# A stabilised linear-attention kernel with a gated feed-forward part: its instruction list ordered anew, with new engines for some 270 steps and new PSUM banks

## The chip, the cores and the metric

One core of a Trainium2 chip runs the whole program. It has a matrix engine (PE, with PEld for its weight loads), a vector engine (DVE), a scalar engine (ACT), a general engine (POOL), and a queue engine (SP) that here only issues transfers. All transfers run on the core's 16 DMA engines. Every engine takes its own instructions strictly in the order in which they are written, and semaphores hold an instruction until what it needs is there. The metric is the time of one execution on the device in microseconds (us); a lower time is better.

## The reference

For 4 batches of 8 heads, 768 time steps and a head size of 40 the first part is a recurrence with exponential gates. The second takes the result as rows of 320 numbers, and computes a gate by a causal convolution of 5 taps, a product with a weight matrix, and a product with a second one.

```python
for t in range(S):
    m_new = np.maximum(f_gate[:, :, t] + m, i_gate[:, :, t])
    f_stab = np.exp(f_gate[:, :, t] + m - m_new)
    i_stab = np.exp(i_gate[:, :, t] - m_new)
    m = m_new
    C = f_stab[:, :, None, None] * C + i_stab[:, :, None, None] * np.einsum('bhd,bhe->bhde', vt, kt)
    n = f_stab[:, :, None] * n + i_stab[:, :, None] * kt
    h_tilde = np.einsum('bhde,bhe->bhd', C, qt)
    denom = np.maximum(np.abs(np.einsum('bhd,bhd->bh', n, qt)[:, :, None]), 1.0)
    o = 1.0 / (1.0 + np.exp(-o_gate[:, :, t]))
    y[:, :, t] = o * h_tilde / denom
# x: y as [batch, time, 320]; xp: x with 4 rows of zeros ahead
gate_pre = sum(conv_w[k] * xp[:, k:k + S, :] for k in range(5))
out = (1 / (1 + np.exp(-gate_pre)) * (x @ w_val)) @ w_out
```

## The kernel before

The 768 steps are cut into 6 tiles (j) of 128 rows, each tile into 4 batches (b). A unit u = 4j + b covers one batch of a tile, with its 8 heads side by side, and has two halves of 64 steps, g = 2u and 2u + 1. Inside a half the recurrence is written as matrix products; between halves a state of 40 x 41 numbers per head is carried on.

The program is one long list, `PLAN`, of 1447 steps. A step such as `probs.18=V` names a function, its numbers and its engine (V for DVE, A for ACT, P for POOL, S for SP), and `scores.18#5` names a matrix step and the PSUM bank (0 to 7) that it writes. The functions are called in the order of the list, and each engine gets its instructions in that order. The list alone decides the order of work, which of several engines does a copy or an elementwise step, and which of the eight banks a matrix step fills. No planner runs when the kernel is built.

The steps that the change and the later sections touch, with the lines of the profile:

- Loads on SP: `ldq` (L390) and `ldk` (L394) bring q and k of a tile into `nat`, `ldv` (L403) brings v into `vc` (`ldv.j.0` for the first half, `ldv.j.1` for the second), `ldo` (L406) the output gate, `wld` (L775) the weights. `sog`, `soa`, `sig_` and `sia` (L443 to L460) carry the cumulated gates through DRAM into `ra` and `la`.
- Splitting q and k: `mx` (L469, ACT) takes the largest value, `scs` (L480 to L485, DVE) makes a scale, `hi` (L497, L499, L501) and `lo` (L506, always DVE) write a high and a low half-precision part into one of three `stk` buffers.
- Turning them: for tiles 0 and 1 PE transposes (`trp`, L523) and `trc` (L527) copies out of PSUM. For tiles 2 to 5 it is `trd` (L518), a transposing transfer on SP, 32 in all: one for q into `tq` and one for k into `tk` for every unit.
- A half g: `args` (L543, PE), `expo` (L547, ACT), `scores` (L555, PE, reads `tk` and `tq`), `probs` (L560, DVE), `keyw` (L568, DVE or POOL), `heads` (L595, PE, reads `vc`), `state` (L578, PE), `stout` (L587, copies the state into `vc`).
- A unit: `norm` (L610 to L615), `rsm` (L619), `gate` (L622, DVE), which ends the attention of a unit; `xeh`, `xel` (L633, L637) split a piece of it, `xtr` (L644, L646, PE) turns it, and `xhc`, `xcc`, `x3c`, `xlo` (L659 to L671) copy and split it.
- The second part, by tile: `cva`, `cvp` (L694, L700) and `cv3` (L708, L710) for the convolution, `sigm` (L721) for the gate, `val` (L731, PE), `zmul` (L736), `zhi` and `zlo` (L740, L745), `outp` (L753, PE), `obc` (L757) into one of two `ob` buffers, and `od` (L760), which stores it. For the last tile, steps from `cva` to `zlo` run in two parts of two batches.
- Weights: `wcv` (L789 to L803), `whi` and `wlo` (L816 to L834) turn the loaded 64-bit weights into two parts; `cpk` (L399) copies k into `kp`.

The choice of engine and bank lies in the loop that ends the function:

```python
for step in PLAN.split():
    step, _, b_ = step.partition("#")
    step, _, e = step.partition("=")
    name, *num = step.split(".")
    steps[name](int(b_) if b_ else e, *(int(n) if n.isdigit() else n for n in num))
```

Of the kernel before, what the change touches and what calls it, by code (L numbers as in the profile page):

```python
# [34 lines left out]
ldv.0.0=S mx.1.0.1=A ldq.2.1=S wcv.0.5=A ldo.0=S trp.0.1.1#5 trp.0.1.0#6 trp.0.2.1#7 ldk.2.0.2=S trc.0.1.0=V args.1#0
trc.0.1.1=V args.0#2 args.2#3 scs.0.0.2.2.3.3=V scs.0.0.2.1.2.3=V scs.0.0.2.3.4.3=V trp.0.2.0#1 zcmp.1.0=V
scs.1.0.2.0.4.0=V scs.0.0.2.1.2.2=V scs.0.0.2.3.4.2=V scs.0.0.2.2.3.2=V scs.1.0.2.0.4.1=V expo.1=A wcv.0.3=V
hi.1.1.1=P trp.0.3.0#4 expo.2=A hi.1.0.1=A args.3#6 keyw.2=P scores.2#5 trc.0.3.0=V scores.1#0 expo.0=A zcd.1=P
args.5#3 wld.1.1=S probs.2=V trc.0.2.1=A wcv.0.4=P scores.0#4 wcv.5.6=V heads.2#2 keyw.0=P lo.1.0.1=V chh=A expo.5=A
# [867 lines left out]
```

## Time and profile before

| | |
|---|---|
| three runs | 241.88, 243.8, 245.06 us; median 243.8 us |
| the profiled execution | 244.12 us, of which the span of its instructions is 242.3 us |
| busy share of the span | DVE 88%, PE 84%, ACT 71%, POOL 53% |
| DMA engines, busy share from 50 to 178 us | 1.18 |

The busy share of an engine is the time with an instruction in it, over the span. A DMA share over 1 means that packets of more than 16 transfers overlap. The chain of waits follows the work that ended last back to the start, and gives at each step what released it. `SPq` in a row is the time that the queue engine spent on issuing a transfer.

### The profile page before, as it was taken

The page shows a single profiled execution, that of the slowest core. Times are in us where ns is not written, and L with a number is a line of the kernel's source. Part 1 is how long each engine was busy: PE and PEld are TensorE (multiplying, and loading weights), DVE is VectorE, ACT ScalarE, POOL GpSimd, SP SyncE. Part 2 cuts the span into 40 slices and gives each one's busy share as a digit, 9 for nine tenths or more (in the row PEclk, how much of TensorE's full clock was granted, in tenths as well). Part 3 has the DMA queues.
Part 4 walks back from the last instruction along what each step waited for, and adds up shares of the span by engine and source line. Part 5 has one row for each costly group of instructions (what it writes and reads, how often), then busy time and mean ns, then how long its engine had stood idle before and what let it go on. Part 6 is the DMA issues. An engine that isn't in the chain of part 4 may idle for free.

```text
span 242.3 us, 6769 instructions
## 1 busy us (share of the span) xinstructions
PE 202.8 (84%) x2544; PEld 171.6 (71%) x2544; DVE 212.7 (88%) x459; ACT 171.9 (71%) x407; POOL 128.4 (53%) x209
## 2 busy tenths in 40 slices
PE   0079469987887699889997985999989989999994
PEld 0045368976776687667965974986879768898994
DVE  7999839999999669996999998897899989998982
ACT  7987928968988569894888965965958268536331
POOL 8942717658968873876766634123518112615330
PEclk9999979999999679995999999999999999999999
DMA  7998897699899999999899999999940330010223
GB/s 122 156 190 122 125 157 146 122 155 146 136 183 148 159 173 172 154 153 167 152 167 164 131 224 167 168 168 221 130 101 4 88 86 27 0 43 14 81 84 108
DMA packets 143832, 31.58 MB, mean 130 GB/s; under 512 B 139576, under 2 KB 142840, under 8 KB 143800
## 3 DMA queue, kind: packets, MB, share of 16 engines
q1 hardware_dynamic: 143696, 31.05, 84.4%
q8 instruction: 20, 0.33, 0.6%
q14 instruction: 12, 0.10, 0.1%
q10 hardware_dynamic: 104, 0.10, 0.1%
HBM read 17.87 MB, written 4.23 MB: 91 GB/s over the span
## 4 chain that ended last, share of the span: by engine, by line
PE 39%; DVE 32%; DMA 9%; ACT 6%; issue 6%; SPq 5%; POOL 1%; DVEq 0%; ACTq 0%; POOLq 0%
PE bank L595 9%; PE bank L753 9%; PE bank L731 6%; DVE stk L506 5%; PE bank L578 5%; DVE pk L560 4%; PE bank L710 3%; DVE sg L736 3%; SPq L394 2%; DMA la<-gda 2%; PE bank L555 2%; DMA vc<-in_v_dram 2%; PE bank L543 2%; DMA tk<-stk 2%; DMA raw<-in_moe_w_val_dram 2%
## 5 line engine op out<-in xcount | busy, mean ns | idle before, releaser
L595 PE MATMUL bank<-vc,pk 128*64 128x41 f32 (+1 forms) x768 | 57.0, 238 | 8.5 <-DMA vc<-in_v_dram 3.6
L595 PEld LDWEIGHTS bank<-vc,pk 128*64 128x64 f32 (+1 forms) x768 | 51.5, 145 | 13.0 <-ACT dm L547 4.0
L578 PE MATMUL bank<-vc,pk 128*40 128x41 f32 (+1 forms) x704 | 38.1, 212 | 1.3 <-DVE xc L663 0.7
L568 POOL TENSOR_TENSOR pk<-kp,dm 128x320 f32<-128x320 f32 (+1 forms) x32 | 25.8, 807 | 22.8 <-ACT dm L547 13.8
L560 DVE SCALAR_TENSOR_TENSOR pk<-bank,cmp,dm 128x512 f32<-128x512 f32 x48 | 34.7, 739 | 3.3 <-PE bank L555 2.2
L578 PEld LDWEIGHTS bank<-vc,pk 128*40 128x40 f32 (+1 forms) x704 | 33.1, 126 | 4.6 <-POOL cdt L863 1.8
L547 ACT ACTIVATE dm<-bank 128x512 f32<-128x512 f32 x48 | 28.0, 597 | 11.1 <-PE bank L543 8.6
L506 DVE SCALAR_TENSOR_TENSOR stk<-nat,scl,stk 128x320 f16<-128x320 f32 x48 | 33.7, 708 | 0.1
L700 DVE SCALAR_TENSOR_TENSOR bank<-xc,cwt,bank 128x512 f32<-128x512 f32 (+1 forms) x42 | 27.8, 671 | 0.6 <-ACT bank L694 0.3
L501 POOL TENSOR_SCALAR stk<-nat,scl 128x640 f16<-128x640 f32 x22 | 18.6, 848 | 14.7 <-issue 6.1
L469 ACT ACTIVATE junk<-nat 128x320 bf16<-128x320 f32 x48 | 22.5, 468 | 2.0 <-DMA nat<-in_k_dram 1.5
L619 POOL TENSOR_TENSOR rs<-sg,den 128x320 f32<-128x320 f32 x17 | 12.4, 735 | 20.8 <-DVE den L615 14.4
L543 PE MATMUL bank<-ra,la 120*128 120x512 bf16 x48 | 18.5, 404 | 5.5 <-DMA la<-gda 2.5
L753 PE MATMUL bank<-woh,zh 128*128 128x320 f32 x72 | 19.3, 324 | 3.7 <-ACT ob L757 2.8
L523 PE MATMUL bank<-idh,stk 128*120 128x128 f16 x128 | 9.8, 232 | 14.2 <-DVE stk L506 13.8
L555 PEld LDWEIGHTS <-tk 120*128 120x128 f16 x384 | 15.6, 102 | 7.1 <-issue 3.6
L555 PE MATMUL bank<-tq,tk 120*128 120x64 f16 x384 | 18.4, 199 | 2.2 <-DMA tk<-stk 0.9
L523 PEld LDWEIGHTS <-stk 128*120 128x120 f16 x128 | 9.1, 144 | 15.1 <-DVE stk L506 14.2
L753 PE MATMUL bank<-wol,zh 128*128 128x320 f32 x72 | 18.4, 309 | 0.0
L587 ACT COPY vc<-bank 40x328 f32<-40x328 f32 x31 | 13.1, 425 | 7.3 <-PE bank L578 6.8
L721 ACT ACTIVATE sg<-sg 128x2816 f32<-128x2816 f32 (+2 forms) x7 | 12.4, 1764 | 7.1 <-DVE sg L700 7.1
L497 ACT ACTIVATE stk<-nat,scl 128x640 f16<-128x640 f32 x20 | 16.2, 825 | 1.1 <-DVE scl L482 0.4
(169 smaller groups left out, 507.1 us busy)
## 6 DMA issues: line engine op xcount, KB each, us to landing
nat<-in_q_dram SPq DMA_DIRECT2D x24, 160.0 KB
vc<-in_v_dram SPq DMA_DIRECT2D x12, 320.0 KB
sg<-in_o_gate_dram SPq DMA_DIRECT2D x6, 640.0 KB
out_dram<-ob SPq DMA_DIRECT2D x24, 160.0 KB
nat<-in_k_dram SPq DMA_DIRECT2D x10, 320.0 KB
raw<-in_moe_w_val_dram SPq DMA_DIRECT2D x5, 160.0 KB
raw<-in_moe_w_out_dram SPq DMA_DIRECT2D x5, 160.0 KB
nat<-in_k_dram SPq DMA_DIRECT2D x4, 160.0 KB
```

What stands on the lines that cost most here:

```text
L469: A.activation(junk, part(j, x, i), AF.Abs, accum_out=amx[j % 2][:, x, i : i + 1])
L506: V.scalar_tensor_tensor(t[:, :, c : c + D], part(j, x, i), scl[j % 2][:, x, i : i + 1], t[:, :, 0:D], op0=ALU.mult, op1=ALU.subtract,)
L523: nc.tensor.transpose(t[0:K3, h], stk[(j * B + i) % NSTK][:, x, h, 0:K3], id16)
L543: nc.tensor.matmul(psd, la[:, p, j % SL, b], ra[:, :, j % SL], start=True, stop=True)
L547: A.activation(dms[g % NDM], late["psd", g], AF.Exp)
L555: nc.tensor.matmul(pss[:, h], tk[h], tq[:, h], start=True, stop=True)
L560: V.scalar_tensor_tensor(pks[g % NPK][:, :, 0:L], late["pss", g], cmp_[j % 2][:, p, b : b + 1], dms[g % NDM], op0=ALU.mult, op1=ALU.mult,)
L568: eng[e].tensor_mul(pks[g % NPK][0:n, :, L:], kp[0:n, p, b * H : (b + 1) * H], dms[g % NDM][0:n, :, L - 1 : L].to_broadcast([n, H, D]),)
L578: nc.tensor.matmul(pc[n0 : n0 + D, h], pks[g % NPK][0:n, h, L:], vc[j % 2][0:n, p, b * H + h], start=True, stop=True)
L595: nc.tensor.matmul(ph[p * L : (p + 1) * L, h], pks[g % NPK][0:n, h, 0:L], vc[j % 2][0:n, p, b * H + h], start=True, stop=True,)
L700: V.scalar_tensor_tensor(o, xc[j % 2][:, c, b0:b1, t : t + P], cwt[:, c, t : t + 1], pv, op0=ALU.mult, op1=ALU.add)
L753: nc.tensor.matmul(po, z, w, start=(i == 0), stop=(i == len(mm) - 1))
```

## The change

`PLAN` alone is replaced: the same 1447 steps in a new order, with the engine of 272 steps and the bank of 268 matrix steps changed. No function, buffer or shape changes. Of the engines' steps 108 leave DVE (54 to POOL, 54 to ACT) and 94 come to it (47 from POOL, 47 from ACT), while 30 pass from POOL to ACT and 30 from ACT to POOL; ten more pass between SP and ACT or POOL, all of them transfers or copies of `kp`.

```diff
 PLAN = """
-zvc.1=P ldf=A ldi=S zkp=V ldq.0.0=S zero.sel=P fsel.0=P ldk.0.0.1=S zero.id=V fsel.1=P zero.tl=V fid=P ldk.0.1.2=S
...
+zrst.1=P ldi=A ldf=S zstk.0=V zkp=V zvc.1=P ldq.0.0=S ldk.0.0.1=S zero.io=P zcmp.0.1=P ldq.0.1=S zero.oh=P
...
```

Three places show what moves.

**The first values of v, on SP.** `L403` loads v of tile 0; the first of the two rows before is `ldv.0.1`, the second `ldv.0.0`. Before:

```order
L449 DMA gda0_141<-gsp0_137 48x1x64
L403 DMA vc0_82<-in_v_dram 64x32x40
L456 DMA ra_86<-gdg0_139 24x8x64
L460 DMA la_85<-gda0_141 24x4x64 x2
L399 DMA kp_81<-nat0_79 64x640
L403 DMA vc0_82<-in_v_dram 64x32x40
L390 DMA nat0_79<-in_q_dram 128x8x40
```

In the change:

```order
L775 DMA raw0_148<-in_moe_w_val_dram 64x640
L456 DMA ra_86<-gdg0_139 24x8x64
L460 DMA la_85<-gda0_141 24x4x64 x2
L403 DMA vc0_82<-in_v_dram 64x32x40 x2
L775 DMA raw1_149<-in_moe_w_val_dram 64x640
```

The two halves now stand together behind the gates, the first half ahead, and the copy of `kp` between them has gone to ACT.

**The transposing transfers of tile 2, on SP.** `stk` holds the split rows, `tq` and `tk` the turned ones that `scores` reads; `nat` is the input of a later tile. Before:

```order
L518 DMA_TRANSPOSE tq0_100<-stk1_109 128x8x128
L518 DMA_TRANSPOSE tq0_100<-stk2_110 128x8x128
L518 DMA_TRANSPOSE tq0_100<-stk0_108 128x8x128
L394 DMA nat1_80<-in_k_dram 128x16x40
L460 DMA la_85<-gda1_142 24x4x64
L394 DMA nat1_80<-in_k_dram 128x16x40
L518 DMA_TRANSPOSE tk0_97<-stk0_108 128x8x128
L518 DMA_TRANSPOSE tk2_99<-stk2_110 128x8x128
L518 DMA_TRANSPOSE tq0_100<-stk2_110 128x8x128
L403 DMA vc0_82<-in_v_dram 64x32x40 x2
```

In the change:

```order
L390 DMA nat1_80<-in_q_dram 128x8x40
L394 DMA nat1_80<-in_k_dram 128x16x40 x2
L390 DMA nat1_80<-in_q_dram 128x8x40
L460 DMA la_85<-gda1_142 24x4x64
L403 DMA vc0_82<-in_v_dram 64x32x40
L518 DMA_TRANSPOSE tk2_99<-stk2_110 128x8x128
L518 DMA_TRANSPOSE tq0_100<-stk2_110 128x8x128
L403 DMA vc0_82<-in_v_dram 64x32x40
L518 DMA_TRANSPOSE tq0_100<-stk0_108 128x8x128
L518 DMA_TRANSPOSE tk0_97<-stk0_108 128x8x128
L460 DMA la_85<-gda1_142 24x4x64
```

The inputs of tile 3 now stand ahead of the first transposing transfer of tile 2, and the transfers for q and k of one unit stand side by side, nearer to the `scores` that read them.

**The last two units, on DVE.** `L622` is `gate`, the end of a unit's attention; behind its last row the engine has only the second part of the layer. Before:

```order
L619 TENSOR_TENSOR rs2_123<-sg_84,den2_120 128x320
L622 TENSOR_TENSOR x2_126<-bank5_73,rs2_123 128x320
L671 TENSOR_TENSOR xl0_596<-xc0_87,xh0_594 128x2x128
L619 TENSOR_TENSOR rs1_122<-sg_84,den2_120 128x320
L757 COPY ob1_131<-bank4_72 128x320
L633 CAST xe2_129<-x2_126 128x64
L700 SCALAR_TENSOR_TENSOR bank7_75<-xc1_88,cwt_96,bank7_75 128x256
L622 TENSOR_TENSOR x1_125<-bank6_74,rs1_122 128x320
L633 CAST xe1_128<-x1_125 128x64
```

In the change:

```order
L619 TENSOR_TENSOR rs1_122<-sg_84,den2_120 128x320
L740 CAST zh_615<-sg_84 128x512
L622 TENSOR_TENSOR x1_125<-bank1_69,rs1_122 128x320
L757 COPY ob0_130<-bank5_73 128x320
L619 TENSOR_TENSOR rs2_123<-sg_84,den2_120 128x320
L622 TENSOR_TENSOR x2_126<-bank2_70,rs2_123 128x320
L700 SCALAR_TENSOR_TENSOR bank7_75<-xc0_87,cwt_96,bank7_75 128x512
```

The two units end closer together, the splitting casts behind them (`L633`) have left DVE, and 50 rows of DVE follow the last `gate` where 45 followed it before.

## Rows read from the trace of the kernel before

**Rows 1.** The page's busy time of each engine with its share of the span, and from its table of 40 equal slices the busy tenths of PE and DVE, of the DMA engines, and the bytes that these moved.

```profile
PE 202.8 (84%) x2544; PEld 171.6 (71%) x2544; DVE 212.7 (88%) x459; ACT 171.9 (71%) x407; POOL 128.4 (53%) x209
...
PE   0079469987887699889997985999989989999994
...
DVE  7999839999999669996999998897899989998982
...
DMA  7998897699899999999899999999940330010223
GB/s 122 156 190 122 125 157 146 122 155 146 136 183 148 159 173 172 154 153 167 152 167 164 131 224 167 168 168 221 130 101 4 88 86 27 0 43 14 81 84 108
```

**Rows 2.** Busy time of each engine in stretches: bounds and length in us, then busy us with the number of instructions for PE, PEld, DVE, ACT and POOL, the granted PE clock, the DMA share, GB/s.

```profile
20.00:40.00 20.00, 15.00 (x212) 12.08 (x211) 14.92 (x36) 13.65 (x27) 9.83 (x14) 0.91 0.97 143
...
50.00:178.00 128.00, 112.57 (x1565) 94.62 (x1563) 114.43 (x242) 100.14 (x242) 77.53 (x117) 0.95 1.18 164
140.00:160.00 20.00, 16.16 (x293) 14.64 (x292) 17.77 (x43) 14.76 (x44) 6.40 (x10) 1.00 1.15 179
...
178.00:242.30 64.30, 59.45 (x562) 52.43 (x559) 55.08 (x118) 31.57 (x74) 20.95 (x30) 0.99 0.18 55
220.00:242.30 22.30, 19.11 (x136) 18.28 (x135) 15.98 (x36) 7.41 (x15) 6.91 (x8) 0.98 0.21 74
```

**Rows 3.** The chain of waits: its shares by engine, and its two longest pieces behind the first tiles that are transfers (start us, us, what).

```profile
PE 39%; DVE 32%; DMA 9%; ACT 6%; issue 6%; SPq 5%; POOL 1%; DVEq 0%; ACTq 0%; POOLq 0%
...
145.85 3.83 DMA out_dram<-ob
...
169.69 4.35 DMA tk<-stk
```

**Rows 4.** The first `heads`: issues on SP and the copy on DVE from the timeline (start us, us, engine, line, what; in brackets the engine's idle time just before and what ended it), then a row of the table of waits (us in total, times, longest).

```profile
20.19 0.67 SPq L403 DMA_DIRECT2D vc<-in_v_dram  x1
...
25.37 0.67 SPq L403 DMA_DIRECT2D vc<-in_v_dram  x1
...
28.55 5.48 SPq L394 DMA_DIRECT2D nat<-in_k_dram  x1
...
36.34 0.92 DVE L587 COPY vc<-bank 40x328 f32<-40x328 f32 x2 [3.94 <-PE bank L578]
...
PE bank L595 <- DMA vc<-in_v_dram: 3.6, 1, 3.6
```

**Rows 5.** Groups by line and shape (line, engine, operation, tiles, shapes, count | busy us, mean ns of one | idle us before and its releasers).

```profile
L506 DVE SCALAR_TENSOR_TENSOR stk<-nat,scl,stk 128x320 f16<-128x320 f32 x48 | 33.7, 708 | 0.1
...
L497 ACT ACTIVATE stk<-nat,scl 128x640 f16<-128x640 f32 x20 | 16.2, 825 | 1.1 <-DVE scl L482 0.4 <-DMA tk<-stk 0.4 <-DMA tq<-stk 0.3
...
L637 POOL TENSOR_TENSOR xe<-x,xe 128x64 fp32r<-128x64 f32 x9 | 4.3, 477 | 8.4 <-DVE xe L633 5.1 <-PE bank L731 3.1
L527 DVE COPY tq<-bank 120x1024 f16<-120x1024 f16 x6 | 4.1, 683 | 0.9 <-PE bank L523 0.8
...
L671 DVE TENSOR_TENSOR xl<-xc,xh 128x256 fp32r<-128x256 f32 x8 | 3.4, 424 | 0.0
...
L637 DVE TENSOR_TENSOR xe<-x,xe 128x64 fp32r<-128x64 f32 x15 | 3.1, 215 | 0.4 <-ACT xe L633 0.3
L499 DVE TENSOR_SCALAR stk<-nat,scl 128x640 f16<-128x640 f32 x6 | 3.1, 545 | 1.0 <-DMA tk<-stk 1.0
...
L399 DVE COPY kp<-nat 64x640 f32<-64x640 f32 x2 | 1.4, 692 | 0.1
...
L799 DVE TENSOR_TENSOR wf<-we,wa 128x320 f32<-128x320 f32 x1 | 0.7, 687 | 0.0
```

**Rows 6.** The low part `lo` on DVE beside POOL, from the timeline (columns as in rows 4).

```profile
29.07 1.08 DVE L506 SCALAR_TENSOR_TENSOR stk<-nat,scl,stk 128x320 f16<-128x320 f32 x1
...
29.08 0.73 POOL L568 TENSOR_TENSOR pk<-kp,dm 128x320 f32<-128x320 f32 x1
...
31.40 0.53 DVE L506 SCALAR_TENSOR_TENSOR stk<-nat,scl,stk 128x320 f16<-128x320 f32 x1
```

**Rows 7.** The transposing transfers: two of tile 2 issued one behind the other and the `scores` that wait for them, from the timeline; then how long one takes SP to issue (min/median/max ns, first and last start us).

```profile
69.62 4.79 SPq L518 DMA_TRANSPOSE tk<-stk  x2
...
77.80 0.41 PE L555 MATMUL bank<-tq,tk 120*128 120x64 f16 x8 [0.88 <-DMA tk<-stk]
...
L518 SPq DMA_TRANSPOSE tq<-stk x16: 1232/1282/4537, 61.6 to 175.2; - x16
L518 SPq DMA_TRANSPOSE tk<-stk x16: 1232/1342/5760, 69.6 to 192.2; - x16
```

**Rows 8.** Sizes of the transfers from the page's list of issues (engine, count, KB each), and the longest wait of ACT and DVE for a store to end (table of waits).

```profile
nat<-in_q_dram SPq DMA_DIRECT2D x24, 160.0 KB
vc<-in_v_dram SPq DMA_DIRECT2D x12, 320.0 KB
sg<-in_o_gate_dram SPq DMA_DIRECT2D x6, 640.0 KB
...
ACT ob L757 <- DMA out_dram<-ob: 3.3, 2, 2.7
...
DVE ob L757 <- DMA out_dram<-ob: 1.4, 1, 1.4
```

More of the change, by code (lines that the diff above doesn't have):

```diff
@@ L35 @@
[L35 to L39, printed above, removed]
@@ L65 @@
-keyw.15=P gate.4=V xtr.2#3 expo.16=A args.18#5 probs.14=V rsm.5=P wcv.2.5=A ldv.2.0=S expo.18=A wcv.2.2=V heads.14#4
-wlo.1.0=P stout.11=V ldv.2.1=S mx.3.3.1=A gate.5=V state.15#7 mx.3.1.1=A xel.3=V lo.2.2.1=V ldk.4.0.2=S heads.15#4
-xhc.2=A wcv.2.3=V keyw.18=P norm.6.0=A xcc.2=V state.13#0 wcv.2.4=V norm.7.0=A xcb.6=A mx.3.0.1=A cpk.2.0.1=P
-scores.18#5 stout.13=V scores.16#6 x3c.2=A xtr.3#2 wcv.2.6=V stout.15=A wld.3.1=S keyw.16=P args.17#0 hi.2.3.1=A
-norm.6.1=V args.19#3 scores.17#7 xeh.4=A xlo.1=P scs.3.0.2.0.4.0=V expo.17=A norm.6.2=V probs.16=V rsm.7=P wld.3.0=S
@@ new lines @@
+ldv.2.0=S xtr.1#2 stout.12=A wcv.2.2=V args.15#3 norm.4.2=V lo.2.0.1=V hi.2.1.0=A scores.13#7 rsm.5=P trd.2.0.1=S
+probs.13=V mx.3.0.1=A rsm.4=P gate.5=V wcv.2.5=A state.14#7 whi.1.0=V expo.15=A cdd.1.0=P heads.13#0 lo.2.1.1=V
+zcd.0=P xcc.0=A gate.4=V mx.3.2.1=A trd.2.0.0=S cdd.1.2=P scores.14#6 keyw.15=P stout.14=A xtr.3#3 probs.14=V
+scores.15#1 xhc.3=A cpk.2.0.0=P args.16#5 xeh.4=A args.17#7 probs.15=V mx.3.1.0=A ldv.2.1=S heads.14#6 xel.4=P xcc.3=A
+keyw.13=V cpk.2.1.0=P expo.17=A lo.2.1.0=V heads.15#6 x3c.1=A xcc.1=A x3c.3=A mx.3.3.1=A stout.11=V trd.2.1.0=S
@@ new lines @@
+wcv.3.5=A ldq.4.1=S sigm.0.0.4=A xel.7=P rsm.8=V wlo.2.2=P ldk.4.0.2=S probs.20=V ldq.4.0=S gate.9=V args.23#6
+gate.8=V heads.20#2 lo.3.1.0=V xeh.8=P lo.3.2.0=V xlo.5=P ldv.3.1=S scores.22#1 zmul.0.1.0.4=V heads.21#2
+zmul.0.0.0.4=V x3b.7=P trd.3.1.0=S keyw.21=P expo.23=A state.22#4 probs.22=V mx.4.1.0=A xlo.4=P scores.23#7
+norm.10.0=A args.26#0 scs.3.1.2.0.4.2=V xel.8=P args.24#5 wcv.3.3=V keyw.23=P xtr.8#6 stout.22=V args.25#1 x3c.8=A
+expo.24=A zmul.0.2.0.4=V state.21#4 cpk.3.1.1=P hi.3.2.1=A probs.23=V scores.24#5 keyw.24=P expo.25=A heads.22#3
@@ new lines @@
+expo.35=A lo.4.3.0=V xlo.11=P heads.34#7 cva.2.1.0.4#0 gate.15=V keyw.35=V state.33#6 stout.34=A zlo.1.1.0.4=P
+sig_.5=S probs.35=V xhc.12=A heads.33#4 zhi.1.2.0.4=V od.0.2=S mx.5.3.0=A state.35#5 stout.33=V trd.4.3.1=S
+norm.16.0=A zlo.1.2.0.4=P heads.35#7 xcc.12=V stout.35=A cvp.2.1.1.0.4=V x3c.12=A mx.5.3.1=A args.38#2 sia.5.0=S
+xlo.8=V cpk.5.1.0=P scores.37#3 args.37#6 norm.17.0=A xeh.14=V od.0.3=S xeh.13=A expo.38=A scores.36#5 outp.1.0#1
+trd.4.3.0=S probs.36=V cva.2.0.0.4#2 keyw.38=P norm.16.1=V expo.37=A xeh.15=P cvp.2.0.1.0.4=V outp.1.1#5 xcb.15=P
@@ L159 @@
+obc.4.2=A zhi.5.0.2.4=V zhi.5.2.2.4=A od.4.2=S outp.5.1#5 zlo.5.2.2.4=P zmul.5.1.2.4=V zlo.5.0.2.4=V zhi.5.1.2.4=A
+outp.5.0#4 obc.5.1=V zlo.5.1.2.4=V od.5.1=S outp.5.3#7 obc.5.0=A od.5.0=S outp.5.2#3 obc.5.3=A od.5.3=S obc.5.2=A
+od.5.2=S
 """
```

249 lines of the change are left out of this document (121 added, 128 removed).

## The prediction

> **What bounds the kernel now.** I read the busy shares first, then the stretches, then the chain of waits, then the prices of the steps that move. The busy shares [rows 1] say that there is not one bound but three that lie close together: DVE is busy 88% of the span, PE 84%, and the DMA engines are full from the start to about 178 us. The stretches make this sharper [rows 2]. From 50 to 178 us PE has 112.6 us of work in 128, DVE 114.4, and the DMA share is 1.18 at 164 GB/s. From 178 us on the DMA engines are nearly idle (0.18), and PE has 59.5 of 64.3 us, DVE 55.1. So there is no engine whose relief alone would bring much: DVE stands idle for 242.3 - 212.7 = 29.6 us in all, PE for 39.5, nearly half of them in the first 40 us, before it has much to do (it is hardly used in the first 20 us by the digits of rows 1, and has 15.0 of the next 20 by rows 2).
>
> The chain [rows 3] is 39% PE, 32% DVE, 9% DMA and 5% the issuing on SP. The last two, 14% or some 34 us, are where a better order can gain most, since the work itself stays the same. Three of its places can be seen in rows. The first values of v hold PE for 3.6 us, and DVE, which waits for the state that follows, for 3.94 us [rows 4]. A store at 145.85 us is on the chain for 3.83 us [rows 3]: `obc` waits up to 2.7 us until it has left the buffer [rows 8], and PE is at 16.2 of 20 us there [rows 2]. A transposing transfer at 169.69 us is on it for 4.35 us [rows 3].
>
> **The change, part by part.** All sums are made against the profiled execution, 244.1 us (a span of 242.3 and 1.8 around it); the median of the three runs, 243.8, lies 0.3 below it.
>
> *Engines.* The work itself changes only where a step changes its engine. Counted by kind, with the mean of the kind on the engine that it leaves or joins, DVE loses a net 11 `xel` at 0.215 us, 2 `trc` at 0.68, 3 `xlo` at 0.42, 2 `hi` at 0.545, 2 `cpk` at 0.69 [rows 5], 2 `zlo` (1.7 us), 3 `zhi`, 4 `xeh`, 2 `obc` and a few more: 14.6 us together. It gains a net 3 `wcv`, one of them at 0.69 us [rows 5], 2 `wlo`, 3 `stout`, 3 `xcc`, 2 gate steps, `ctl` and small ones: 10.3 us. The net is **-4.3 us**. DVE paces most of the program, so I count it in full. ACT gains 2.7 us (five more `hi` at 0.825 [rows 5], two `trc`, less what leaves) and POOL 8.1 us (`xel` costs 0.477 us there [rows 5]). I cost both at nothing, since ACT stands idle for 70 us of the span and POOL for 114 [rows 1]; if that cover were gone on ACT, it would be 2.7 us. ACT changes its table of functions as often as before, since the runs of `expo` and of the sigmoids alternate as often.
>
> *POOL beside DVE.* What moves to POOL is not free for DVE. A `lo` takes 0.53 us alone, and 1.08 us when a `keyw` of 0.73 us starts beside it on POOL [rows 6]; over all 48 the mean is 0.708 us [rows 5], so that 48 x (0.708 - 0.53) = 8.5 us go to this in `lo` alone. Against POOL's 128.4 busy us [rows 1] that is 0.07 us of DVE for each us of POOL; 8.1 us more of POOL give **+0.5 us**. The ends are 0 (the splitting steps that leave DVE no longer wait there) and 8.1 (each us blocks DVE for one). I take the value near the mean, since it is what 48 steps show. [...]
>
> *The first values of v.* Before, `ldv.0.1` goes out at 20.19 us and `ldv.0.0`, which the first `heads` needs, at 25.37 us behind two gate loads and a copy of `kp`; what was asked for up to then is still in the queue, and the next k load holds SP for 5.48 us [rows 4]. In the change `ldv.0.0` is asked for first, one transfer of 320 KB [rows 8] earlier, which at 143 GB/s [rows 2] is 2.2 us. DVE has 7.0 us of its own steps between that issue and the first `heads`, where it had 5 (25.37 to about 30). Gain **-2.0 us**; the bounds are 0 (the queue in front is as long) and -3.9, the whole wait.
>
> *Stores.* `od.0.1` now has 7.5 us of DVE work ahead of the `obc.0.3` that reuses its buffer, against 2.3 before; that wait (up to 2.7 us) should go. But `obc.0.2`, on DVE, has 3.0 us behind `od.0.0` where it had 5.3, and it waited 1.4 us already [rows 8]; it would wait 3.7. **0**, with -2.7 and +2.3 as bounds.
>
> *Transposing transfers.* This is the part that I like least. In the list of before, the last of a unit's two transfers has 3.8 to 14.6 us of DVE work between itself and the `scores` that read it, 8.5 us in the mean over the 16 units; in the change 4.0 to 9.4, and 6.1 in the mean. A transfer takes 4.35 us until it can be read [rows 3]. Before, that is already tight: the pair that SP issues from 69.62 to 74.41 us keeps `scores` waiting for 0.88 us at 77.8 [rows 7]. In the change six units have under 5 us, where two had, and an issue that meets a full queue takes up to 5.76 us where 1.3 is usual [rows 7], 4.5 us more; 5.48 us has happened to a load too [rows 4]. Lower bound 0 (SP keeps up), upper bound 9 us (two of the tight pairs meet such an issue). Nearest is the row of a tight pair that cost 0.88 us; the four further ones make 3.5, some of it hidden by other steps on DVE. I take **+2.0 us**.
>
> *Loads.* By the time at which DVE has done 75 us of its steps, about 78 us in, the list of before has asked for 11.9 MB and the change for 10.7 MB (counts of the transfers by their sizes [rows 8]); at 150 us of DVE work it is 24.7 against 24.2. From 78 to 159 us the change thus asks for 13.5 MB, 166 GB/s; the engines moved 164 in this stage and 179 in the best 20 us of it [rows 2]. I cost it at **0**, with +5 as the bound: 0.9 MB, the mean backlog, at 164 GB/s.
>
> *The end.* The last `gate` has 50 rows of DVE and more of PE's work behind it than before, which means that it comes earlier and that the end has more to fill PE with. PE is idle for 3.2 of the last 22.3 us [rows 2], most of it behind the last product. **0**, bounds -2 and +1.5.
>
> The sum: 244.1 - 4.3 + 0.5 - 2.0 + 2.0 = 240.3 us, and 0.3 less for the median: **240.0 us**, 1.6% below 243.8. With two neighbouring values of the terms exchanged this case lies between 236.5 and 244.
>
> **The rivals.** What a measurement of this kernel can tell from no change is 2%, that is 4.9 us: faster is under 238.9, slower over 248.7.
>
> - *The waits on transfers close up* (0.28). The wait for v goes entirely (-3.9), the stores do not hold PE (-2.7), the transposing transfers stay hidden, and DVE's 4.3 us come through: 244.1 - 4.3 - 3.9 - 2.7 + 0.5 = 233.7; I take 236, since not all of them will. For it: 14% of the chain is transfers and their issue [rows 3]. Against it: PE and DVE are both at 88% from 50 to 178 us [rows 2], so a gap that closes on one soon meets the other.
> - *The transfers come too late* (0.20). With the DMA engines full at 1.18 [rows 2], what is not asked for early cannot be caught up. If the 0.9 MB stay behind, `scores` of tiles 2 to 5 wait at the transposing transfers, and DVE's saved time turns into waiting: 244.1 + 5.5 = 249.6, and more with two blocked issues. It decides from the point where SP runs over 4 us behind its place in the list, since six units have no more than 5 us in between. The rows for it are the wait of 0.88 us [rows 7] and the issues of over 5 us; against it, 179 GB/s were reached from 140 to 160 us. [...]
> - *POOL takes back what DVE gives* (0.07). If each us of POOL blocks DVE for one, DVE has 3.8 us more: 244.1 + 3.8 - 2.0 + 2.0 - 0.3 = 247.6, within 2%. [...] Against it is that only 8.5 us go in `lo` beside 128 us of POOL.
>
> The forecast itself has 0.45. Of the forecast's 0.45 I put 0.10 under 238.9, since its own range reaches below; of the fast rival 0.25; of the late one 0.15 over 248.7 and, of POOL's, 0.02. That gives 0.35 faster, 0.48 the same and 0.17 slower. The range 234 to 249 leaves out about a tenth at either end.
>
> **What would show it.** DVE's busy time should be 208 to 210 us and POOL's near 136. The wait of `heads` for v should be under 2 us, and DVE's idle time before `stout` near 35 us under 2. In the row of `scores`, waits for `tk` or `tq` should add up to 1 to 4 us; over 8 us in `scores`, or `heads` and `probs` late by a like amount in tiles 2 to 5 with SP behind, would show the late rival. [...] The last `gate` should end near 207 us, where it ended at 215. I am wrong if DVE's busy time falls as counted and the time does not: then the gaps, not the work, decide, and the order of the list has made new ones.

## The result and the profile after

The change takes 234.16 us at the median of four runs (230.56 to 237.81), beside 242.84 us for the kernel before (240.99 to 245.06). The ratio is 0.9554 with a 95% interval of 0.9447 to 0.966. Two repetitions, on two chips, gave medians of 234.8 and 234.54 us. That is 3.6% less by the medians and 4.5% by the ratio, which compares the faster runs of each kernel alone; 240.0 us, 1.6% less, was forecast.

The granted clock is the share of PE's full clock that the profile records as granted. In the traces of before and after it is 1.00 or 0.50 at any time: 0.50 for 20.5 us of the change's 236.0, in stretches of 3.4 and 17.1 us, and for 18.1 of the 242.3 us of before. By its mean over the run, the change's 17 runs in this study lie on two levels of time: 230.6 to 232.7 us with 0.99 to 1.00, and 234.4 to 237.8 us with 0.956 to 0.971, and none lies between. The execution with the profile (237.81 us, a span of 236.0) is on the upper level.

First the page of the change: busy time and share of each engine, then PE, DVE, the granted PE clock and the DMA engines in 40 slices of 5.9 us [rows 1].

```profile
PE 207.9 (88%) x2544; PEld 175.3 (74%) x2544; DVE 205.2 (87%) x447; ACT 174.2 (74%) x411; POOL 135.2 (57%) x217
...
PE   0039799998988889869999999999999999999994
...
DVE  7899979999999999957379998989999997899770
...
PEclk9999979999999999985579999999999999999999
DMA  7986996998999998999898379989986710004033
```

DVE has 205.2 us of work where it had 212.7, and POOL 135.2 where it had 128.4. From the 19th slice on PE is at 9 tenths to the end, where five slices of 5 to 8 stood in between before [rows 1]. The dip is in slices 18 to 21: the clock falls, and DVE falls with it to 3 tenths.

The stretches [rows 2] (columns as there) say the same in us.

```profile
20.00:40.00 20.00, 18.42 (x242) 14.05 (x240) 17.95 (x53) 15.81 (x34) 5.40 (x8) 0.91 1.02 150
50.00:178.00 128.00, 120.22 (x1628) 100.67 (x1627) 113.68 (x238) 104.97 (x251) 90.46 (x140) 0.93 1.04 155
140.00:160.00 20.00, 19.50 (x277) 16.39 (x276) 18.36 (x40) 14.89 (x45) 13.36 (x19) 1.00 1.08 176
178.00:236.00 58.00, 54.79 (x488) 49.28 (x485) 46.41 (x101) 28.54 (x70) 17.98 (x26) 1.00 0.28 73
100.00:120.00 20.00, 17.82 (x179) 15.31 (x178) 11.99 (x28) 12.23 (x37) 8.99 (x14) 0.60 1.03 168
```

From 20 to 40 us DVE has 17.95 us of work, where it had 14.92; from 140 to 160 us PE has 19.50, where it had 16.16. The one bad stretch is 100 to 120 us, at a granted clock of 0.60: DVE does only 11.99 us of work in 20.

Prices on DVE by shape [rows 5], first of the change, then, for `zlo` (L745), which was not shown, of the kernel before.

```profile
L506 DVE SCALAR_TENSOR_TENSOR stk<-nat,scl,stk 128x320 f16<-128x320 f32 x48 | 30.3, 642 | 2.5 <-ACT stk L497 2.4
...
L745 DVE TENSOR_TENSOR zh<-sg,zh 64x512 fp32r<-64x512 f32 x2 | 2.0, 977 | 0.4 <-ACT zh L740 0.4
...
L745 DVE TENSOR_TENSOR zl<-sg,zh 128x256 fp32r<-128x256 f32 x4 | 1.7, 414 | 0.0
L745 DVE TENSOR_TENSOR zl<-sg,zh 128x512 fp32r<-128x512 f32 x2 | 1.4, 718 | 0.0
```

```profile
L745 DVE TENSOR_TENSOR zl<-sg,zh 128x512 fp32r<-128x512 f32 x5 | 4.9, 980 | 0.0
...
L745 DVE TENSOR_TENSOR zh<-sg,zh 64x512 fp32r<-64x512 f32 x3 | 2.8, 932 | 0.0
L745 DVE TENSOR_TENSOR zl<-sg,zh 128x256 fp32r<-128x256 f32 x3 | 1.7, 581 | 0.3 <-ACT zh L740 0.3
```

The same `lo`, 48 of them on DVE in both kernels, is cheaper: 0.642 us against 0.708 [rows 5], 3.2 us together. Part of that is the one profile: three later kernels whose list is that of before but for a step or two (v first, useless products, gates earlier) have it at 0.650 to 0.662.

```profile
L506 DVE SCALAR_TENSOR_TENSOR stk<-nat,scl,stk 128x320 f16<-128x320 f32 x48 | 31.0, 650 | 0.3
L506 DVE SCALAR_TENSOR_TENSOR stk<-nat,scl,stk 128x320 f16<-128x320 f32 x48 | 31.3, 658 | 0.1
L506 DVE SCALAR_TENSOR_TENSOR stk<-nat,scl,stk 128x320 f16<-128x320 f32 x48 | 31.5, 662 | 0.1
```

The seven profiles with the list of the change, or one a step or two from it, have 0.625 to 0.642; so `lo` by itself gives back some 1 to 3 us. The mean `zlo` of 128x512 fell from 0.980 us (five of them) to 0.718 (two), that of 128x256 from 0.581 to 0.414.

Beside what these instructions are longer can be read from the traces one by one. The 16 `lo` of before that no POOL instruction overlaps took 0.534 to 0.550 us, the other 32 0.791 in the mean; in the change 13 took 0.537 to 0.552, and the other 35 0.678. Of the five `zlo` of 128x512 of before three took 0.68 to 0.69 us, and two, with POOL at work beside them, 1.26 and 1.58; one of the three had POOL beside it too, so not every meeting costs. It is so for DVE as a whole: in every kept trace the instructions that meet no POOL instruction (122 to 185 of them) lie within 0.02 us of the median of their shape, but for one or two. Those that meet one are longer than that median by 16.8 us in all in the kernel before (15.4 to 17.1 in the three kernels near it) and by 13.3 in the change (10.9 to 13.9 in the seven profiles). These sums are estimates from the traces; 15 to 21 instructions of each, of shapes that hardly occur without POOL, are left out. One kind did not pay: `probs` (L560) took 0.739 us beside POOL and 0.737 without it in the kernel before, and none took over 0.752.

Then the waits of the change: engine, line, what it waited for, us in total, times, longest.

```profile
PE bank L555 <- ACT dm L547: 2.0, 1, 2.0
...
PE bank L555 <- DMA tk<-stk: 0.7, 1, 0.7
...
DVE stk L506 <- ACT stk L497: 2.4, 1, 2.4
...
ACT junk L469 <- DMA nat<-in_q_dram: 5.3, 2, 4.1
ACT ob L757 <- DMA out_dram<-ob: 4.8, 3, 2.0
```

The wait of `heads` for v, 3.6 us before [rows 4], has no row any more. New are a wait of 2.0 us of `scores` (L555) for `expo` (L547), one of 2.4 us of `lo` for `hi` on ACT (L497), and one of ACT at `mx` (L469) for a load of q. The timeline of ACT, and behind it that of PE, shows that the three are one event (start us, us, engine, line, what; in brackets the idle time before and its end).

```profile
97.42 0.60 ACT L547 ACTIVATE dm<-bank 128x512 f32<-128x512 f32 x1
102.14 0.47 ACT L469 ACTIVATE junk<-nat 128x320 bf16<-128x320 f32 x1 [4.12 <-DMA nat<-in_q_dram]
...
102.81 0.61 ACT L547 ACTIVATE dm<-bank 128x512 f32<-128x512 f32 x1
103.30 0.84 ACT L497 ACTIVATE stk<-nat,scl 128x640 f16<-128x640 f32 x1
```

```profile
100.69 0.81 PE L578 MATMUL bank<-vc,pk 104*40 104x41 f32 x16 [0.20 <-DVE vc L587]
103.47 0.39 PE L555 MATMUL bank<-tq,tk 120*128 120x64 f16 x8 [1.98 <-ACT dm L547]
```

ACT stands for 4.12 us at `mx.4.1.0`, the largest value of a piece of q of tile 4, whose load has not landed. Behind it in ACT's queue is `expo.24`, which has to empty the bank that `scores.24` fills, and behind that the `hi` that `lo` needs. From 103.9 to 121.0 us PE is at half of its clock; a product of `heads` takes 0.305 to 0.309 us there in the mean, and 0.230 from 122 to 160 us.

### The profile page after: what moved, and what is told of

It reads as the page before. It is cut to its first block, busy times and chain, and to the rows that moved or that the text cites. A ratio compares the mean times of both kernels' runs of the same rounds, so it can differ in the third digit from the quotient of the medians.

```text
span 236.0 us, 6770 instructions
## 1 busy us (share of the span) xinstructions
PE 207.9 (88%) x2544; PEld 175.3 (74%) x2544; DVE 205.2 (87%) x447; ACT 174.2 (74%) x411; POOL 135.2 (57%) x217
## 5 line engine op out<-in xcount | busy, mean ns | idle before, releaser
L595 PE MATMUL bank<-vc,pk 104*64 104x41 f32 (+1 forms) x768 | 56.8, 239 | 0.3
L595 PEld LDWEIGHTS bank<-vc,pk 104*64 104x64 f32 (+1 forms) x768 | 51.6, 147 | 5.7 <-issue 2.2
L578 PE MATMUL bank<-vc,pk 128*40 128x41 f32 (+1 forms) x704 | 36.9, 209 | 3.0 <-DVE pk L560 1.0
L560 DVE SCALAR_TENSOR_TENSOR pk<-bank,cmp,dm 128x512 f32<-128x512 f32 x48 | 35.1, 742 | 3.5 <-PE bank L555 3.2
L578 PEld LDWEIGHTS bank<-vc,pk 128*40 128x40 f32 (+1 forms) x704 | 32.1, 124 | 7.0 <-POOL pk L568 2.5
L506 DVE SCALAR_TENSOR_TENSOR stk<-nat,scl,stk 128x320 f16<-128x320 f32 x48 | 30.3, 642 | 2.5 <-ACT stk L497 2.4
L547 ACT ACTIVATE dm<-bank 128x512 f32<-128x512 f32 x48 | 28.2, 597 | 4.1 <-PE bank L543 3.4
L469 ACT ACTIVATE junk<-nat 128x320 bf16<-128x320 f32 x48 | 22.6, 471 | 7.9 <-DMA nat<-in_q_dram 5.3
L501 POOL TENSOR_SCALAR stk<-nat,scl 128x640 f16<-128x640 f32 x19 | 17.2, 908 | 13.6 <-issue 7.3
L523 PE MATMUL bank<-idh,stk 128*120 128x128 f16 x128 | 10.8, 238 | 14.9 <-DVE stk L506 14.9
L619 POOL TENSOR_TENSOR rs<-sg,den 128x320 f32<-128x320 f32 x18 | 14.0, 785 | 16.5 <-ACT sg L625 8.5
L555 PE MATMUL bank<-tq,tk 120*128 120x64 f16 x384 | 18.6, 197 | 5.0 <-ACT dm L547 2.0
L555 PEld LDWEIGHTS <-tk 120*128 120x128 f16 x384 | 15.1, 100 | 9.4 <-issue 5.9
L497 ACT ACTIVATE stk<-nat,scl 128x640 f16<-128x640 f32 x25 | 20.3, 826 | 0.7 <-DVE scl L482 0.3
L745 POOL TENSOR_TENSOR zl<-sg,zh 128x512 fp32r<-128x512 f32 x8 | 10.5, 1313 | 13.9 <-ACT zh L740 11.7
L543 PE MATMUL bank<-ra,la 120*128 120x512 bf16 x48 | 17.8, 400 | 0.6 <-DVE pk L560 0.2
L587 ACT COPY vc<-bank 40x328 f32<-40x328 f32 x28 | 11.9, 425 | 8.3 <-PE bank L578 7.1
```

The source lines that it names most:

```text
L469: A.activation(junk, part(j, x, i), AF.Abs, accum_out=amx[j % 2][:, x, i : i + 1])
L497: A.activation(o, s, AF.Copy, scale=f)
L506: V.scalar_tensor_tensor(t[:, :, c : c + D], part(j, x, i), scl[j % 2][:, x, i : i + 1], t[:, :, 0:D], op0=ALU.mult, op1=ALU.subtract,)
L523: nc.tensor.transpose(t[0:K3, h], stk[(j * B + i) % NSTK][:, x, h, 0:K3], id16)
L547: A.activation(dms[g % NDM], late["psd", g], AF.Exp)
L555: nc.tensor.matmul(pss[:, h], tk[h], tq[:, h], start=True, stop=True)
```

## The experiments

**Engines alone, and the order alone.** The list of before with the engines of the change, and the list and banks of the change with the engines of before. 272 steps differ in each.

```diff
 the list of before
-... xel.1=V xel.3=V xel.2=P ...
+... xel.1=P xel.3=P xel.2=V ...
```

> The list of before with its banks, with the engine of every step as in the change: the engines alone. Theory A (the work that leaves DVE is what counts): DVE's busy time falls from 212.7 to about 208 us and the time by 3 to 5 us, to 238 to 240. Theory B (the order closes waits, the engines only fit that order): DVE's busy time falls as well, but the time stays within 2 us of before or rises, 241 to 246, since steps stand on engines that are busy at their place in this order.

> The list and banks of the change with the engine of every step as before: the order alone. Theory A: 240 to 244 us, since DVE has its 4.3 us back. Theory B: most of the gain of the change is here, 232 to 237 us, with the wait for v at the first heads gone and the last gate before 207 us.

The first takes 256.86 us, a ratio of 1.0479 (1.0325 to 1.0634); the second 258.38 us, 1.0589 (1.0479 to 1.0698). The busy rows of the two pages, of the engines alone and then of the order alone, and the longest wait of POOL in the second:

```profile
PE 209.8 (82%) x2544; PEld 177.5 (70%) x2544; DVE 211.2 (83%) x447; ACT 175.3 (69%) x411; POOL 129.9 (51%) x217
```

```profile
PE 213.9 (83%) x2544; PEld 178.8 (70%) x2544; DVE 218.1 (85%) x459; ACT 173.7 (68%) x407; POOL 130.4 (51%) x209
```

```profile
POOL rs L619 <- DVE den L615: 25.0, 7, 7.3
```

Both expectations of each run are missed, by some 11 us or more. Neither half is worth anything alone: each loses 5 to 6%, and together they gain. The shares show how. DVE's busy share falls to 83 and 85%, so it is waits that come back, on POOL too, whose `rsm` waits 25.0 us in all for a step of DVE, where it was 14.4. In the order alone DVE also has 5.4 us more work than before.

**v first, in the kernel before.**

```diff
+ldv.0.0=S
 ldv.0.1=S
 ...
-ldv.0.0=S
```

> The kernel before with one load moved: ldv.0.0 goes out just ahead of ldv.0.1 on SP, as in the change, and nothing else. If the wait for v in the first heads (3.6 us on PE, 3.9 on DVE) is worth what the first stage shows, the first gates come 2 to 3 us earlier and the time falls by 2 to 3 us, to 239 to 241. If what is won there is taken back by the next wait (DMA engines full from 50 us on), the first gates come earlier and the time stays within 1 us of before.

243.72 us, a ratio of 1.0009 (0.996 to 1.0059): nothing. The wait for v is gone, but this is PE's row for the gates in this kernel, where it was 2.5 us in all before:

```profile
PE bank L543 <- DMA la<-gda: 6.0, 2, 4.8
```

The first half of v now stands ahead of the loads of the gates, which `args` (L543) waits for. The wait changed its name.

**The splitting steps back, in the change.** `xel`, `xlo` and `zlo` on the engines of before, 36 steps.

```diff
-xel.1=P xel.3=P xel.2=V
+xel.1=V xel.3=V xel.2=P
```

> The change with the 36 splitting subtractions xel, xlo and zlo whose engine it changed put back on the engine of before (net 16 come back to DVE, and 10 us leave POOL). If POOL's added work costs DVE little (0.07 us for each us), DVE's busy time rises by 5 us and the time by 2 to 5. If POOL blocks DVE for most of each us, lo gets shorter than in the change and the time stays the same or falls.

235.93 us (234.78 to 237.13), all four runs with a clock of 0.985 or more, so it is to be set beside the lower level of the change: some 4 us slower. DVE has 210.5 us of work, 5.3 more than the change:

```profile
PE 201.8 (87%) x2544; PEld 169.7 (73%) x2544; DVE 210.5 (90%) x463; ACT 174.3 (75%) x411; POOL 126.4 (54%) x201
```

**The same steps, in the kernel before.** The mirror of it, run later.

> The kernel before with the engines of the change for xel, xlo and zlo alone (36 steps, 26 from DVE to POOL and 10 the other way; the mirror of the run that put them back in the change and lost 3.5 us). If these steps' engines are worth their DVE time wherever they stand, DVE's busy time falls by about 5 us and the time by 3 to 4 us, to 239 to 240. If engines only pay in the order that they were found with, it stays or rises, as all 272 did (11 to 14 us slower): 243 to 246.

244.5 us, 1.0084 (1.0033 to 1.0135). The page's busy row, and two of its rows of `zlo` on DVE:

```profile
PE 203.1 (84%) x2544; PEld 170.8 (71%) x2544; DVE 212.7 (88%) x443; ACT 172.0 (71%) x407; POOL 137.6 (57%) x225
```

```profile
L745 DVE TENSOR_TENSOR zh<-sg,zh 64x512 fp32r<-64x512 f32 x2 | 2.6, 1292 | 0.1
L745 DVE TENSOR_TENSOR zl<-sg,zh 128x512 fp32r<-128x512 f32 x2 | 2.3, 1156 | 0.0
```

This is the clearest pair of the study. Sixteen steps net leave DVE, and it is busy for 212.7 us, as before (profiles of nearly the same list differ by up to 1.6 us in this). What they took there comes back as longer instructions, such as the two `zlo` of 128x512 that stay: 1.156 us in the mean, with POOL beside both all the way, instead of 0.980. The length that DVE's instructions gain beside POOL, by the estimate above, rises from 16.8 to 21.1 us, mostly in small steps such as those of `scs` and `wcv`, while `lo` fell to 0.666 us. In the order of the change the same move is worth 5.3 us of DVE: with the steps back that length is 14.9 us, where it is 13.3 with them moved.

**What POOL costs DVE.** The change with 32 useless POOL products.

```diff
+def pad(e, n):
+    eng[e].tensor_mul(padt, padt, padt)
...
-lo.2.0.1=V
+pad.0=P lo.2.0.1=V
```

> The change with 32 useless POOL products of 128x320 numbers, one ahead of each `lo` of tiles 2 to 5 in the list, some 25 us of POOL work more. It measures what POOL costs DVE for each us. The prediction's rate (0.07 us of DVE for each us of POOL) expects 2 us more of DVE busy time, 207 us, and `lo` (L506) at 0.66 us in the mean. [...] Its time is of less interest, since POOL's own steps come later too: 235 to 250 us.

The page's busy row, then POOL's row of the products and DVE's of `lo` (L509 here, since lines were added ahead of it):

```profile
PE 207.7 (87%) x2544; PEld 174.6 (73%) x2544; DVE 212.0 (89%) x447; ACT 174.4 (73%) x411; POOL 164.0 (69%) x250
```

```profile
L874 POOL TENSOR_TENSOR padt<-padt 128x320 f32<-128x320 f32 x32 | 26.7, 834 | 0.9
...
L509 DVE SCALAR_TENSOR_TENSOR stk<-nat,scl,stk 128x320 f16<-128x320 f32 x48 | 32.8, 692 | 0.9 <-POOL stk L504 0.7
```

The one run took 241.14 us. POOL has 28.8 us more, DVE 6.8 us: 0.24 us for each, over three times the rate of the prediction, and a quarter of its other end, at which each us of POOL blocks DVE for one; neither came. `lo` rose to 0.692 us, which is 2.4 us of the 6.8. What DVE's instructions gain in length beside POOL goes from 13.3 to 20.2 us by the estimate above, which is the whole of it.

**The change again, and v late in it.**

> The change itself once more, to have a profile in which PE's granted clock is not at half for 17 us from 103.9 us on, as it is in the first profile of the change. Both theories expect a span of 229 to 231 us. The theory of work (the change gains because DVE's instructions became cheaper) expects DVE's busy time near 205 us again, with `lo` (L506) near 0.64 us, and DVE idle for about as long as before, 27 to 30 us. The theory of gaps (the change gains because waits closed) expects DVE's idle time at 24 us or less, against 29.6 before.

234.8 us (232.72 to 236.67), 0.9751 (0.9681 to 0.9821). Its profile, too, is on the upper level: 234.9 us of span, DVE busy for 205.0 and idle for 29.9. That is the idle time that the theory of work expects, but some 5 us of it belong to the bad stretch, so it decides nothing; four profiles at the lower level, of kernels a step or two away, have 25.2 to 27.1, which fits neither theory well. It shows the bad stretch in closer steps (columns as in [rows 2]):

```profile
110.00:120.00 10.00, 10.00 (x83) 7.89 (x83) 5.91 (x15) 5.92 (x22) 4.39 (x7) 0.53 1.12 154
```

PE is busy for all of these 10 us, at about half of its clock, and DVE has 5.91.

```diff
+ldv.0.1=S
 sig_.0=S
 ...
-ldv.0.0=S
 ldv.0.1=S
+ldv.0.0=S
```

> The change with the second half of v of tile 0 asked for ahead of the gates and the first half behind, so that what `heads` needs first leaves one transfer later, as before. The prediction's term (one transfer of 320 KB, 2 us) expects 2 us more than the change and a wait of heads (L595) of about 2 us for in_v_dram. The theory that the first wait is only passed on to what comes next (nothing came of the same move in the kernel before) expects no more than 0.7 us.

236.6 us (232.46 to 238.79), on both levels. The one run with a clock of 0.993 took 232.46 us, inside the change's lower level, and its profile has no wait of `heads` for v. The 2 us of the prediction's term cannot be seen there, though one run doesn't exclude 1 us, and the other three lie some 1 us above the mean of the change's upper level (237.3 against 236.1).

This profile shows something else. It is on the lower level, and yet ACT waits as long for the load of q as in the profile of the change (first row). What differs is PE: its clock was at half from 99.6 to 103.0 us, its work ahead of `scores.24` took longer for that, and `scores.24` waited 0.32 us instead of 1.98 (second row). No further stretch at half clock follows.

```profile
102.43 0.47 ACT L469 ACTIVATE junk<-nat 128x320 bf16<-128x320 f32 x1 [4.12 <-DMA nat<-in_q_dram]
103.76 0.39 PE L555 MATMUL bank<-tq,tk 120*128 120x64 f16 x8 [0.32 <-ACT dm L547]
```

So the wait on ACT alone does not make the upper level. This run, in which PE hardly stood still behind it, is on the lower one; the runs with one load moved and with useless products, below, test that.

**Half of the engines back, in the change.**

> The change with the engines of before for the 117 steps that stand ahead of gate.9 in the list and differ (the prologue, tiles 0 and 1, a part of 2). All engines of before in this order cost 10.6% (26 us over the change). If the engines and the order have to fit at every place, about 117 of 272 steps should cost 117/272 of that, 11 us. If the loss of that kernel came from one stage, this run or its sister has nearly all of the 26 us and the other under 4.

> The sister of the run before: the change with the engines of before for the 155 steps that differ from gate.9 on (tiles 2 to 5 and the second part of the layer). Fit everywhere: about 155/272 of 26 us, 15 us. Loss in one stage: nearly 26 us or under 4 us. The theory of work would give both runs only what their own steps cost on DVE, together about 5 us.

244.98 us, 1.0168 (1.0086 to 1.0249), and 244.41 us, 1.0142 (1.0041 to 1.0242). Both lose about 10 us against the change, so the loss does not sit in one half of the list. But they lose it in different coin, as the busy rows show, of the first half and then of the second:

```profile
PE 208.7 (85%) x2544; PEld 175.3 (72%) x2544; DVE 208.0 (85%) x437; ACT 173.6 (71%) x412; POOL 140.1 (57%) x225
```

```profile
PE 205.7 (86%) x2544; PEld 172.1 (72%) x2544; DVE 214.4 (89%) x469; ACT 174.7 (73%) x406; POOL 124.1 (52%) x201
```

In the first (a span of 245.1 us) DVE works 208.0 us and stands idle for 37.1: the old engines make waits. In the second (240.5 us) it works 214.4 us and is idle for 26.1: they make work.

**One load at the head of ACT's queue.**

```diff
-mx.4.1.0=A
 ...
 expo.24=A
 ...
 hi.3.2.1=A
 ...
 expo.25=A
 ...
 hi.3.3.1=A
 ...
 cpk.3.0.1=A
 ...
+mx.4.1.0=A
```

Of ACT's steps, `norm.10.0` and `x3c.8` stand in the first gap: the step moves behind seven steps of ACT in all.

> The change with mx.4.1.0 four steps of ACT later, behind expo.24, hi.3.2.1, expo.25, hi.3.3.1 and the copy of k. In the run of the change again ACT waits 4.2 us at this step for the load of q of tile 4, expo.24 stands behind it, scores.24 waits 1.97 us for its bank, and DVE 2.4 us for hi.3.3.1; then PE's clock is at half for 17.1 us. Theory 'a load at the head of ACT's queue' expects the wait of L555 for dm to be gone, no half-clock stretch of over 4 us near 102 us, and 230 to 231 us in nearly all runs (4 us under the change again). Theory 'the wait passes on' (SP and the DMA engines set the pace up to there) expects scores of the next unit to wait instead, and 234 to 235 us.

231.99 us (231.65 to 233.75), 0.9564 (0.9522 to 0.9606). Run again with the change beside it on one chip:

> The change beside the next run on one chip. With the load of q at the head of ACT's queue the theory expects runs at two levels, with a half-clock stretch of 3 or of 17 us near 102 us: 231 to 233, and 235 to 238.

> The change with mx.4.1.0 four steps later on ACT, beside the run before this one. The theory expects one level, 231.5 to 234 us, and a lower median than the change by 1 to 4 us. If the gain of the first run of it was the chip's, both have the same median within 1 us.

The change has 234.54 us (231.19 to 237.12), in six runs three at 231.2 to 232.4 and three at 236.7 to 237.1. With the step moved it is 231.7 us (231.38 to 232.78), and of ten runs in two studies none lies above 233.75. From the stretches of the second profile (span 229.6 us):

```profile
20.00:40.00 20.00, 19.11 (x276) 14.28 (x275) 18.96 (x56) 17.68 (x36) 5.55 (x9) 1.00 1.05 157
...
178.00:229.60 51.60, 48.36 (x393) 43.25 (x391) 39.67 (x88) 23.43 (x57) 14.23 (x20) 1.00 0.22 66
80.00:100.00 20.00, 17.14 (x184) 13.67 (x185) 18.13 (x37) 15.93 (x29) 15.41 (x27) 0.93 1.24 178
100.00:120.00 20.00, 18.77 (x295) 15.43 (x294) 17.19 (x37) 17.42 (x52) 12.44 (x21) 0.99 1.05 168
```

From 100 to 120 us DVE has 17.19 us of work where the change at its upper level has 11.99. The 5.2 us between them are about the distance of the two levels (4.4 us between their means over all 17 runs, 5.2 in the six beside this kernel). The wait for the load did not pass on. This kernel, one step of 1447 from the change, is the best of the study: it removes the upper level, and takes nothing off the lower.

**The clock without the wait.** The wait is left as it is, and useless products fill PE's gap.

```diff
+def spin(b_, n):
+    for _ in range(n):
+        nc.tensor.matmul(bank(b_, P), id16, id16, start=True, stop=True)
...
+spin.32#3
 scores.24#5
```

> The change with 32 useless products of 128 columns ahead of scores.24 on PE, in the bank that heads.22 fills next, so that PE works through the gap of 1.97 us while the wait of scores.24, of DVE and of ACT stay. It tells the price of the clock from that of the wait. If the clock is the price, the half-clock stretch of 17 us goes and the run is near 231 us. If the wait is, the run stays at 234 to 236 us, with the clock up.

232.84 us (231.44 to 233.53), 0.9581 (0.9529 to 0.9633), with clocks of 0.991 to 1.000. ACT still waits for the load, and the stretch behind it is at the full clock (two answers of one kernel):

```profile
ACT junk L469 <- DMA nat<-in_q_dram: 4.0, 1, 4.0
```

```profile
100.00:120.00 20.00, 19.14 (x315) 16.09 (x313) 17.20 (x36) 16.94 (x52) 12.47 (x21) 1.00 1.15 170
```

So most of the price is the clock's. A wait of 4 us on ACT and of 2 us on DVE, with PE kept at work, costs about 1 us at the end (232.84 against 231.7 to 232.0). The half clock that follows the gap costs the rest of the distance, some 3 to 4 us (the mean of the upper level is 236.1).

**The same, and the gates earlier, in the kernel before.** 24 such products in the gap of 2.12 us ahead of `heads.16`; and, in a kernel of its own, three gate loads some 20 us earlier.

```diff
+spin.24#3
 heads.16#0
```

```diff
+sia.3.1=S sig_.3=S sia.3.0=S
 wld.3.1=S
 ...
-sig_.3=S
 ...
-sia.3.0=S
 ...
-sia.3.1=S
```

> The kernel before with 24 such products ahead of heads.16 on PE, in the gap of 2.12 us that ends at 81.31 us, ahead of the half-clock stretch from 80.8 to 87.6 us, in which DVE then waits 2.08 and 2.34 us. If that clock is a price of its own, the stretch goes or is 3.4 us, and the time falls by 2 to 4 us against before. If the time is made up later (the waits come back at a transfer), it falls by less than 1 us.

> The kernel before with the three loads of tile 3's gates (sia.3.1, sig_.3, sia.3.0) further up in SP's queue, ahead of wld.3.1, some 20 us earlier; nothing else moves. Before, they are issued from 94.0 to 102.7 us, 4 us ahead of the first args that read them, though their buffer is free from 68.2 us on; in the change two of the three leave at 74 to 76 us and no args waits. If a wait on a transfer that stands too late is worth its length, the wait of L543 for la near 105 us goes and with it the half-clock stretch at 108 us: 2 to 4 us off before, 239 to 241 us. If each wait that is closed in this order opens another (as v moved first did, where the wait for la grew from 2.5 to 6.0 us), the time stays within 1 us of before.

242.79 us, 0.9997 (0.994 to 1.0054), and 243.94 us, 1.0084 (1.0032 to 1.0135). In the first the half-clock stretches only moved, to 77.5 us (3.4 us) and 104.8 us (6.8 us). In the second the wait for `la` near 105 us is gone and so is the stretch at 108 us, but the first `args` of tile 3 still starts at 105.5 us (105.4 before), another stretch stands at 148.5 us, and the kernel is a little slower. In these cases, as with v first, a wait that was closed in this order opened another.

## Why the prediction was wrong

It had the direction right and the size wrong: 240.0 us was forecast, and 231 to 238 came. On the profiles DVE shows where. Before, it worked 212.7 us and stood idle for 29.6. In the profile of the change it works 205.2 us and is idle for 30.8. At the lower level (the two profiles of the kernel one step from the change) it works 204.4 and 202.8 us and is idle for 25.2 and 27.1: 8 to 10 us of work and 2.5 to 4.4 of idle time less. The forecast had 3.8 us of work less and, with +2.0 and -2.0, no idle time.

- *Engines (-4.3) and POOL beside DVE (+0.5): the second is the step that failed.* It took a mean, 0.07 us of DVE for each us of POOL, and multiplied it by the 8.1 us that POOL gains. POOL gained 6.8 to 8.3 us as forecast, and yet what DVE loses to it fell: by the estimate above from 16.8 to 13.3 us, -3.5 where +0.5 was forecast. (With the kernels near each, 15.4 to 17.1 and 10.9 to 13.9, the fall is about 3 us in the mean.) `lo`, from which the mean was taken, has only 7.9 of the 16.8 us and 1 to 3 of the fall. The other 4.0 us by which DVE's work fell are the steps that left it, so the -4.3 was about right. The cost does not go by POOL's total, and not by a rate: the useless products cost 0.24 us for each us, the 36 split steps took back all of their gain in the old order, and none of it in the new one. It goes by which instruction stands beside which. What in such a meeting makes DVE's instruction longer is not shown. The end of 8.1 us, at which each us of POOL blocks DVE for one, was as wrong as my mean, since it, too, counted POOL's us and not the meetings; with the useless products it was a quarter of a us.
- *The first values of v (-2.0).* The wait went, 3.6 us to none, and 20 to 40 us gained 3 to 4 us of DVE's work. But the move alone is worth nothing in the kernel before, and undoing it cost between nothing and some 1 us in the change. The term priced a wait by its length, without asking what is next in the queue; in the old order that was the load of the gates.
- *Transposing transfers (+2.0).* Somewhat too high: `scores` waits 1.0 us for `tk` and `tq` in the profile of the change and 2.5 in the second profile of it, where it was 0.9 [rows 7], so 0.1 to 1.6 us were added. The issues that the prediction laid to a full queue came in the change as before: by sums over the transfers and packets of the two traces (an estimate), the nine issues on SP with over 800 KB asked for and not yet moved took 3.0 to 5.8 us, and those with under 400 KB at most 2.7.
- *Stores (0).* ACT's waits for `out_dram` are 4.8 us where they were 3.3 [rows 8], DVE's 0.8 where they were 1.4; small, as forecast.
- *Loads (0), and ACT's work at nothing.* Here a whole effect was missed. In bytes the loads nearly kept up (155 to 161 GB/s from 50 to 178 us, where it was 164). One of them, a piece of q, came 4.1 us late for a step at the head of ACT's queue. I had named ACT's idle 70 us as cover; here they were no cover for what stood behind a step that waited 4.1 us. The rival of the late transfers looked for this at the 32 transposing ones, six of them tight, and it was a plain load for a tile that nobody needed yet. The load was issued at 96.7 us in the second profile of the change, and ACT stood ready for it 0.4 us later (at 97.1), 4.2 us ahead of its landing.
- *The clock.* No term of the sum had it. Before, PE was at half from 33.0, 80.8 and 108.1 us on, 17 us together, and DVE stood idle for 2.08 and 2.34 us in the second of these. In both profiles with `mx.4.1.0` moved it is 3.4 us, and in the second of them DVE's idle time from 80 to 100 us is 1.9 us instead of 4.95. Whether the clock is a cause of that or follows from it is not shown: useless products in the gap of before gained nothing.
- *The end (0).* The last `gate` ended at 203.0 us in the profile of the change and at 196.4 in the second one with `mx.4.1.0` moved, against 215.6 before, earlier than the 207 forecast. But 33 us follow it, where it was 27; PE is busy for 48.4 of the 51.6 us from 178 us on.

Of the rivals, the first, in which the waits close up at 236 us, was nearest in time, by other means than it named: the idle time fell by 2.5 to 4.4 us at the lower level, and not at all at the upper one, while most of the gain is DVE's work. It is luck that the median lies just inside the range of 234 to 249: the runs on the upper level put it there, by an effect that the prediction did not have, and the lower level lies outside. My rule for being wrong, that DVE's work falls as counted and the time does not, was the opposite of what happened.

What stays open is where the rest of the fit lies. The runs show that both halves of the list have a part in it, that it needs both order and engines, and in what coin each half loses. They do not name the single waits. That a gap on PE is what lowers the clock is shown at one place, ahead of `scores.24`: from 100 to 120 us the clock is 0.60 behind the gap of 1.98 us and 1.00 with products in it. How long the clock then stays low is open: with the splitting steps back a gap of the same length, ahead of `args` in this row, preceded only 3.4 us at half.

```profile
81.97 0.38 PE L543 MATMUL bank<-ra,la 120*128 120x512 bf16 x1 [1.98 <-DVE pk L560]
```

## What to carry to other kernels

An order and its engines are one object: parts of a jointly found schedule must not be priced, or taken over, one by one. A step that moves from DVE to POOL is priced by the instructions that it will stand beside (here 36 moved steps left DVE's 212.7 us as they were in one order and were worth 5.3 us in the other), and a wait by what is queued behind it, on every engine, also on one with much idle time (here 4.12 us on ACT). Where runs lie on two levels, look for the first gap on PE ahead of the place where the granted clock falls (here 1.98 us ahead of 17.1 us at 0.50), and for a step that waits for a transfer with nothing urgent behind that transfer.
